# A Fourier-mixing and feed-forward block: which instruction takes a fresh pair of accumulator banks, and about 300 pieces at other places in the order

## The chip, the cores and the metric

One core of a Trainium2 chip runs one program. The metric is its time on the device in microseconds (us), as a median of several runs; beside it stands one profiled execution, whose rows are quoted throughout. Engines are named as in the profile: PE (TensorE: matrix products), DVE (VectorE), ACT (ScalarE), POOL (GpSimd), SP (SyncE: it issues transfers). The accumulators (PSUM) are eight banks of 128 x 512 floats; the kernel takes them in pairs, four pairs in all, one after another in turn.

## The reference

One transformer block in float32: a Fourier mixing layer and a feed-forward layer, each on a normalised input and each added to its input. x is 2048 x 512; the sequence matrices are 2048 x 2048, the hidden ones 512 x 512, w1 is 512 x 1792 and w2 1792 x 512.

```python
def _A_ref(x, dft_seq_re, dft_seq_im, dft_hid_re, dft_hid_im):
    a = jnp.einsum("bsd,ed->bse", x, dft_hid_re)
    b = jnp.einsum("bsd,ed->bse", x, dft_hid_im)
    return jnp.einsum("ts,bse->bte", dft_seq_re, a) - jnp.einsum("ts,bse->bte", dft_seq_im, b)

def _B_ref(x, w1, w2):
    h = _silu(jnp.einsum("bsd,df->bsf", x, w1))
    return jnp.einsum("bsf,fd->bsd", h, w2)

h = x + _A_ref(_layernorm(x), ...)
h2 = h + _B_ref(_layernorm(h), B_w1, B_w2)
```

## The kernel before, in words

**Arithmetic.** A float32 number is split in two parts of lower precision: ScalarE rounds it (`ph`, made at line 263), VectorE subtracts to get the remainder (`pl`, lines 267 and 269). Each product is then three matmuls into one bank: high x high, high x low, low x high (`three`, lines 313 to 315). The matrix products are made as Strassen-Winograd products: of a two-by-two block product, seven products (numbered 1 to 7 in the code) of sums of blocks, where VectorE makes the sums (line 711, `sub`) or a transfer adds on the way (`plus`, `prep`), and the results are added up partly in the banks and partly by VectorE.

**Stages.** The sequence transform comes first (`plain`, `fast`; banks `c` and `m`), for two halves of the output; `mix_fast` then multiplies by the hidden matrices (banks `y`), adds the residual (line 832) and calls `norm_h`, which normalises by way of a GpSimd reduction over partitions (line 903). `make_w2` splits the second layer's weights beforehand and stores them. Then, for each half q, `up` makes the first layer of the feed-forward part and `down` the second (banks `f`, weights fetched at line 1169).

**The first layer.** `up(q, ...)` goes over seven pairs p of hidden blocks. A pair has a bank Y (the first half of a bank pair `y`) and the banks V and X (the two halves of a bank pair `vx`). Products 1, 6, 5 and 3 go into Y, 7 and 4 into V, 2 into X. Product 1 is also needed as the start of X, so ScalarE copies Y into X when product 1 is done; product 2 then accumulates on it, and product 6 on Y. One product is six matmuls. The order is 1, 7, 6, 2, 5 for the first pair and, for every later one, 1, 7, 3 (of the pair before), 6, 2, 4 (of the pair before), 5. What follows each product (`post`) is on ScalarE or VectorE: `silu` (line 1065), `copy` (1068), `add` (1071), and the copy into X (1079).

**Order.** Nothing is ordered by hand in the text of the stages. Each stage appends pieces to a list `events`, every one with a planned time: matmul steps one behind another at 0.2265 us a matmul, other pieces at a lead before or a delay behind their step. The n-th piece appended has the number n. At the end the list is sorted by planned time plus the number that the table `MOVED` has for n:

```python
return sorted(((t + MOVED.get(n, 0.0), at, n, f) for t, at, n, f in events), key=lambda v: v[:3])
```

At the same time, what follows a step (0) comes before other pieces (1) and those before a step (2). In this order the instructions are traced, and each engine keeps the order in its own queue, SyncE's and GpSimd's transfers included. Buffers (51 pages of 128 x 1024 floats in SBUF, four pairs of banks) are handed out in the same order; the first instruction to use a buffer waits until its former contents have been read, and waits are put in from the order in which instructions use buffers. In the profile ScalarE's copy is the first to use a `vx` pair, since `post(1)` takes the pair and copies at once, and `post(1)` comes before the step of product 7, at the same planned time.

Pieces that the text speaks of, by number: 160 (the splits `S` of three sums of the input), 224 (the remainder of a hidden matrix, line 807), 269, 325, 629 and 696 (remainders `pl` of sequence blocks or their sums), 829 (transfers of parts of w2) and 830 (four subtractions on these, lines 1138 to 1141), 931 and 1247 (transfers of w1, line 991), 988 (the copy into X of the fifth pair, first half).

Of the kernel before, what the change touches and what calls it, by code (L numbers as in the profile page):

```python
# [42 lines left out]
FREE_US = {None: 2.0, "matmul": 4.0, "dma_start": 10.0}  # L43
LATE_SUMS = 2, 3, 4, 5, 6
# [200 lines left out]
def program(nc, page, keep, small, psum, dram, x, xT, seq, hid, ffn, out):  # L245
# [11 lines left out]
    def banks(name):  # L257
        return psum.tile([P, 2, 512], F32, tag="ps", name=name)
# [74 lines left out]
    X, xc, xraw = {}, {}, {}  # L333
# [713 lines left out]
    def up(q, lead, between):  # L1047

        bank = {}
# [9 lines left out]
        def mm(n, p):  # L1059
            if n == 1:  # L1060
                bank[p, "Y"] = banks(f"y{q}{p}")[:, 0, :]
            mul(n, p, n in (1, 7), n in (2, 6, 5, 3, 4))
# [323 lines left out]
```

## Time and profile before

| | |
|---|---|
| median of 3 runs | 685.56 us (684.73 to 687.5) |
| the profiled execution's own time | 684.68 us |
| its span, first to last instruction | 682.6 us |
| TensorE busy | 662.9 us, 97% of the span, 2892 matmuls |
| VectorE busy | 574.9 us, 84% |
| ScalarE busy | 372.0 us, 54% |
| mean granted TensorE clock | 0.999 |
| moved by transfers | 184.22 MB, mean 270 GB/s |

The span is what the rows of the trace cover; some 2 us of the device time lie around it. An engine is busy while one of its instructions runs; a matmul's row lasts longer than the distance to the next one, since matmuls overlap. Rows of a timeline are: start, duration, engine, line, operation, output and inputs, shapes, and in brackets the idle time of the engine before it with what ended it. In rows of a stretch each engine has its busy time and its number of instructions.

### The profile page before, as it was taken

What the parts mean: (1) busy time and instruction counts of PE and PEld (TensorE: products, weight loads), DVE (VectorE), ACT (ScalarE), POOL (GpSimd) and SP (SyncE); (2) the same over time, 40 slices, a digit from 0 to 9 for tenths busy, and PEclk for the clock granted to TensorE, in tenths of its full rate; (3) what the DMA queues carried; (4) which work ended last, traced back from release to release, by engine and by line L of the source; (5) the groups of instructions that cost most, each with busy time, mean ns of one, the idle gap of its engine ahead of it and who ended that gap; (6) DMA issues with size and microseconds to landing.
All of it is one profiled execution on the core that took longest, in us unless ns stands there. A gap on an engine that the chain in (4) does not pass through costs nothing.

```text
span 682.6 us, 8286 instructions
## 1 busy us (share of the span) xinstructions
PE 662.9 (97%) x2892; PEld 540.5 (79%) x2892; DVE 574.9 (84%) x727; ACT 372.0 (54%) x476; POOL 98.1 (14%) x128
## 2 busy tenths in 40 slices
PE   9999999999999999999999999989999999999996
PEld 6888887878888888888888877768888777778885
DVE  7899978998989999999999998967998545279874
ACT  6996555654545444455666446775455445554600
POOL 0010112120003233011201034341000000000000
PEclk9999999999999999999999999999999999999999
DMA  8975899999896769899999995459988562268803
GB/s 318 359 179 150 249 323 358 278 306 323 297 368 258 266 184 283 303 349 371 384 304 403 333 355 212 174 216 302 348 313 331 178 226 98 82 231 298 328 31 124
DMA packets 59706, 184.22 MB, mean 270 GB/s; under 512 B 6800, under 2 KB 13840, under 8 KB 59664
## 3 DMA queue, kind: packets, MB, share of 16 engines
q1 hardware_dynamic: 45456, 132.79, 53.7%
q0 software_dynamic: 13920, 50.63, 23.5%
q8 instruction: 23, 0.38, 0.2%
q10 hardware_dynamic: 288, 0.26, 0.1%
q14 instruction: 19, 0.16, 0.1%
HBM read 139.34 MB, written 44.32 MB: 269 GB/s over the span
## 4 chain that ended last, share of the span: by engine, by line
PE 87%; DVE 4%; DMA 3%; ACT 3%; issue 2%; SPq 0%; POOL 0%; DVEq 0%; ACTq 0%
PE m L314 8%; PE m L315 8%; PE m L313 8%; PE y L314 7%; PE y L315 7%; PE y L313 7%; PE f L315 6%; PE f L314 6%; PE f L313 6%; PE c L313 3%; PE c L314 3%; PE c L315 3%; PE vx L313 3%; PE vx L314 3%; PE vx L315 3%; DMA raw<-in_seq 3%
## 5 line engine op out<-in xcount | busy, mean ns | idle before, releaser
L263 ACT ACTIVATE ph<-raw 128x1024 fp32r<-128x1024 f32 x102 | 105.5, 1055 | 84.4 <-DVE raw L711 18.5
L267 DVE TENSOR_TENSOR pl<-raw,ph 128x1024 fp32r<-128x1024 f32 x88 | 109.0, 1257 | 7.9 <-ACT ph L263 7.4
L314 PE MATMUL m<-pl,S 128*128 128x512 f32 x192 | 74.8, 390 | 0.8 <-DVE pl L267 0.8
L315 PE MATMUL m<-ph,S 128*128 128x512 f32 x192 | 74.7, 389 | 0.0
L313 PE MATMUL m<-ph,S 128*128 128x512 f32 x192 | 74.7, 389 | 0.0
L313 PE MATMUL f<-gth,wf 128*128 128x512 f32 x161 | 62.6, 389 | 0.0
L314 PE MATMUL f<-gtl,wf 128*128 128x512 f32 x161 | 62.6, 389 | 0.0
L315 PE MATMUL f<-gth,wf 128*128 128x512 f32 x161 | 62.6, 389 | 0.0
L263 ACT ACTIVATE gth<-g 128x1024 fp32r<-128x1024 f32 x42 | 42.8, 1053 | 34.2 <-DVE g L1200 30.0
L1071 DVE TENSOR_TENSOR g<-vx,g 128x512 f32<-128x512 f32 x28 | 19.3, 690 | 48.3 <-PE vx L315 34.2
L314 PE MATMUL m<-pl,X 128*128 128x512 f32 x144 | 56.1, 390 | 1.0 <-DVE pl L267 1.0
L267 DVE TENSOR_TENSOR gtl<-g,gth 128x1024 fp32r<-128x1024 f32 x42 | 50.5, 1220 | 7.6 <-ACT gth L263 5.0
L315 PE MATMUL m<-ph,X 128*128 128x512 f32 x144 | 56.0, 389 | 0.0
L313 PE MATMUL m<-ph,X 128*128 128x512 f32 x144 | 56.0, 389 | 0.0
L711 DVE TENSOR_TENSOR raw<-raw,raw 128x1024 f32<-128x1024 f32 x36 | 47.8, 1331 | 1.6 <-DMA raw<-in_seq 1.3
L314 PE MATMUL y<-pl,hf 128*128 128x512 f32 x112 | 43.7, 390 | 0.0
L313 PE MATMUL y<-ph,hf 128*128 128x512 f32 x112 | 43.6, 389 | 0.0
L315 PE MATMUL y<-ph,hf 128*128 128x512 f32 x112 | 43.6, 389 | 0.0
L314 PEld LDWEIGHTS m<-pl,S 128*128 128x128 f32 x192 | 36.0, 188 | 8.9 <-DVE pl L267 1.4
L313 PEld LDWEIGHTS m<-ph,S 128*128 128x128 f32 x192 | 36.0, 188 | 7.5
L315 PEld LDWEIGHTS m<-ph,S 128*128 128x128 f32 x192 | 36.0, 188 | 7.4
L314 PEld LDWEIGHTS f<-gtl,wf 128*128 128x128 f32 x161 | 30.2, 188 | 6.3
(399 smaller groups left out, 1540.3 us busy)
## 6 DMA issues: line engine op xcount, KB each, us to landing
raw<-in_seq SPq DMA_DIRECT2D x84, 512.0 KB, 6.6
hf<-fd SPq DMA_DIRECT2D x28, 512.0 KB, 6.1
wf<-wd SPq DMA_DIRECT2D x28, 512.0 KB, 6.7
wf<-wd SPq DMA_DIRECT2D x28, 384.0 KB, 4.3
sf<-sd SPq DMA_DIRECT2D x18, 512.0 KB, 7.0
raw<-in_seq POOLq DMA_DIRECT2D x16, 512.0 KB, 6.9
fd<-hf POOLq DMA_DIRECT2D x14, 512.0 KB, 6.4
w<-in_ffn SPq DMA_DIRECT2D x23, 256.0 KB, 6.7
```

The source lines that it names most:

```text
L263: nc.scalar.activation(hi, src, AF.Copy, scale=sign)
L267: nc.vector.tensor_tensor(lo, src, hi, op=ALU.subtract)
L313: nc.tensor.matmul(acc, wh, mh, start=first, stop=False, skip_group_check=on)
L314: nc.tensor.matmul(acc, wh, ml, start=False, stop=False, skip_group_check=on)
L315: nc.tensor.matmul(acc, wl, mh, start=False, stop=last, skip_group_check=on)
L711: nc.vector.tensor_tensor(o, a, b, op=ALU.subtract)
L1071: nc.vector.tensor_tensor(g[q, f][:, tau, :], src, g[q, f][:, tau, :], op=ALU.add)
```

## The change

The pair of banks `vx` is taken when the step of product 7 is traced, by its first matmul, and no longer by ScalarE's copy. The copy of product 1 into X (`post(1)`) is planned 0.05 us behind product 1's end, so that it comes behind the step of product 7 in the order. Besides, 325 entries of `MOVED` have another value, come in or go out; the matmul steps have the same order as before.

```diff
+SEED_US = 0.05
...
         def mm(n, p):
             if n == 1:
                 bank[p, "Y"] = banks(f"y{q}{p}")[:, 0, :]
+            if n == 7:
+                t = banks(f"vx{q}{p}")
+                bank[p, "V"], bank[p, "X"] = t[:, 0, :], t[:, 1, :]
             mul(n, p, n in (1, 7), n in (2, 6, 5, 3, 4))
...
             if n == 1:
                 for i in range(2):
                     g[q, 2 * p + i] = page(f"g{q}{p}{i}")
-                t = banks(f"vx{q}{p}")
-                bank[p, "V"], bank[p, "X"] = t[:, 0, :], t[:, 1, :]
                 nc.scalar.activation(bank[p, "X"], bank[p, "Y"], AF.Copy)
...
-            after = [(0, lambda n=n, p=p: post(n, p))]
+            after = [(SEED_US if n == 1 else 0, lambda n=n, p=p: post(n, p))]
```

Of `MOVED`, the entries that the text speaks of (us, added to the planned time):

| piece | before | after |
|---|---|---|
| 160 | 27.45 | 21.61 |
| 224 | -0.48 | 9.8 |
| 269 | 7.52 | 1.26 |
| 325 | 7.54 | 5.83 |
| 629 | 0.53 | 7 |
| 696 | 6.8 | 7.94 |
| 829 | -0.65 | -10.88 |
| 830 | 0.56 | -11.76 |
| 931 | -77.43 | -54.39 |
| 988 | -0.38 | 2.42 |
| 1247 | none | -56.42 |

207 rows, old and new, of the table MOVED are left out of this document.

## The prediction

> **What bounds the kernel now.** I read the page's busy times first, then TensorE's waits, then the timeline around the commonest wait, then busy time by stage.
>
> ```profile
> PE 662.9 (97%) x2892; PEld 540.5 (79%) x2892; DVE 574.9 (84%) x727; ACT 372.0 (54%) x476; POOL 98.1 (14%) x128
> PEclk9999999999999999999999999999999999999999
> ...
> PE vx L313 <- ACT vx L1079: 11.0, 14, 1.5
> PE m L314 <- DVE pl L267: 1.8, 2, 1.0
> ...
> 200.00:300.00 100.00, 100.00 (x442) 82.65 (x442) 95.02 (x105) 49.59 (x53) 29.04 (x26) 1.00 0.82 275
> 300.00:400.00 100.00, 99.33 (x438) 81.72 (x438) 97.92 (x110) 56.76 (x63) 15.00 (x26) 1.00 1.00 358
> 400.00:500.00 100.00, 94.97 (x413) 76.70 (x412) 84.18 (x133) 61.06 (x88) 31.58 (x36) 1.00 0.74 269
> ```
>
> TensorE is the bound: 97% busy at full granted clock. It issues 442 matmuls in 100 us where nothing stops it, one each 0.226 us, so time can only come out of its gaps. Nearly all of them are one wait, 14 times, once for each pair of hidden blocks in each half of the first layer: the seventh product (`vx`) waits for ScalarE's copy at line 1079. Second comes VectorE: 95 to 98% busy from 200 to 400 us, so there a remainder (`pl`) that comes late is TensorE's next wait. Two such waits exist already.
>
> ```profile
> 404.06 0.39 PE L314 MATMUL y<-T1l,wah 128*128 128x512 f32 x1
> 404.29 0.39 PE L315 MATMUL y<-T1h,wal 128*128 128x512 f32 x1
> 404.72 0.58 ACT L1079 ACTIVATE vx<-y 128x512 f32<-128x512 f32 x1 [0.76 <-PE y L315]
> 405.35 0.50 PE L313 MATMUL vx<-T7h,sf 128*128 128x512 f32 x1 [0.67 <-ACT vx L1079]
> 405.69 0.39 PE L314 MATMUL vx<-T7l,sf 128*128 128x512 f32 x1
> ```
>
> This is one of the 14. The first product's last matmul starts at 404.29 and ends at 404.68, the copy runs from 404.72 to 405.30, and the seventh product starts at 405.35. The copy writes X, the product writes V, the other half of the same pair of banks: no data passes between them. The product waits because the copy is the first user of the newly taken pair.
>
> **The change, part by part.** *The 14 waits.* From 404.29 to 405.69 are 1.40 us for two issues that take 0.45 undisturbed: 0.95 lost, of which the waits view counts 0.67 as idle; the slow restart and the drain are 0.28 more. Over all, 11.0 + 14 x 0.28 = 14.9 us. Now the product takes the pair, and I expect the order of first users to turn round: the copy waits for the product's first matmul. That would start at 404.29 + 0.23 = 404.52 and end at 404.91; the copy would run from 404.95 to 405.53. The next matmul that needs the copy done is the sixth product, which accumulates on Y. In the first pair of each half it follows the seventh at once, at 404.52 + 6 x 0.226 = 405.88: 0.35 us to spare. In the other 12 the third product of the pair before lies between, and 1.7 us are spare. So I take all 14 waits as gone: -14.9.
>
> Two things could put some of it back. ScalarE works in order:
>
> ```profile
> 397.44 1.05 ACT L263 ACTIVATE T4h<-hn 128x1024 fp32r<-128x1024 f32 x1
> ...
> 457.63 0.62 ACT L1065 ACTIVATE g<-g 128x512 f32<-128x512 f32 x1
> ...
> 401.68 1.22 DVE L832 TENSOR_TENSOR h<-y,h 128x1024 f32<-128x1024 f32 x1
> ```
>
> An activation of 1.05 us that has just begun delays the copy by up to that, hidden 12 times by the 1.7 us, and costing up to 0.7 in each of the two first pairs. The long wait of 1.5 us was such a queue (the activation at 457.63 ahead of the copy). The copy of the fifth pair (piece 988, offset -0.38 to 2.42) now stands 2.47 us behind its first product, still ahead of the sixth product at 12 x 0.226 = 2.71. If the copy waits for the whole seventh product, it ends 0.58 + 0.04 after that one's end and the two first pairs stand as long as now: 2 x 0.95 = 1.9. Bounds for this term are 0 and +1.9; I take 0, for a wait at 404.72 came 0.04 us behind the one matmul it needed. What is late next in place of the copy is the bank itself: the second pair's banks are read last by the residual sum at 401.68, done at 402.90. That pair's product could now start at 404.52 less the 0.95 gained in the first pair, 403.57: 0.67 spare, nothing added.
>
> The Trainium skill (PSUM — Partial Sum Buffer, Terms) forbids two engines on one bank at one time, an error and not a delay. Copy and seventh product touch three different banks, so by that rule they may overlap and the term stays 0; were the pair guarded as one, it would be +1.9. The trace agrees only in part: the wait above exists between two different banks, so it comes from the program's hand-over of the pair.
>
> *The moved pieces.* 325 offsets differ; most shift work that has spare time. TensorE's own order of products is untouched. I compared the order of each queue in the two tables, SyncE's and GpSimd's loads and stores too, and looked for remainders that lose their lead.
>
> ```profile
> 112.70 1.22 DVE L267 TENSOR_TENSOR pl<-raw,ph 128x1024 fp32r<-128x1024 f32 x1
> 113.98 0.50 PE L314 MATMUL m<-pl,X 128*128 128x512 f32 x1 [1.01 <-DVE pl L267]
> ...
> 148.63 0.69 DVE L807 TENSOR_TENSOR hf<-hid,hf 128x512 fp32r<-128x512 f32 x1
> 149.23 1.22 DVE L267 TENSOR_TENSOR pl<-raw,ph 128x1024 fp32r<-128x1024 f32 x1
> ...
> 150.51 0.50 PE L314 MATMUL m<-pl,S 128*128 128x512 f32 x1 [0.83 <-DVE pl L267]
> ...
> 151.50 1.89 DVE L406 TENSOR_TENSOR S<-s,S 128x512 fp32r<-128x512 f32 x3
> ...
> 301.25 2.35 DVE L267 TENSOR_TENSOR pl<-raw,ph 128x1024 fp32r<-128x1024 f32 x2
> ...
> 305.72 0.39 PE L314 MATMUL m<-pl,X 128*128 128x512 f32 x1
> ...
> 315.88 0.43 DVE L1138 TENSOR_TENSOR v<-u,v 128x256 f32<-128x256 f32 x1 [1.58 <-DMA v<-in_ffn]
> ...
> 344.85 1.22 DVE L267 TENSOR_TENSOR pl<-raw,ph 128x1024 fp32r<-128x1024 f32 x1
> 345.99 0.95 DVE L406 TENSOR_TENSOR wal<-w,wah 128x768 fp32r<-128x768 f32 x1
> ...
> 346.52 0.39 PE L314 MATMUL m<-pl,X 128*128 128x512 f32 x1
> ```
>
> Each of the two old waits costs its idle time and 0.28: 1.29 and 1.11, mean 1.2. Piece 269, the remainder at 112.70, comes 6.3 us earlier (7.52 to 1.26): its wait goes, -1.3 (bounds -1.3 and 0). Piece 325, the one at 149.23, gets piece 160's three subtractions (1.89 us, 27.45 to 21.61) ahead of it and loses piece 224 (0.69, at 148.63, now 10.3 later): its wait grows by 1.2 (bounds 0 and 1.9). Piece 629, second of the two at 301.25, ends at 303.60 and is needed at 305.72, 2.1 spare; it moves 6.5 later (0.53 to 7), behind piece 830's four subtractions (the first at 315.88, which stood 1.58 waiting for its load), drawn 12.3 earlier with that load, piece 829. Piece 696, at 344.85, has 0.45 spare and gets the `wal` remainder ahead of it, whose load (piece 931) now starts 23 us later. For 629 and 696 no row shows the new order; the bounds are 0 (load early) and 1.9 (as for 325), and I take one ordinary wait each, 2 x 1.2 = 2.4.
>
> In the first layer VectorE was busy 84.18 of 100 us; about 7 pairs there lose 0.95 each, so it would be 84.18 of 93.4, 90%: below what 200 to 400 us carry at full TensorE. No term there.
>
> **Sum.** -14.9 + 0 - 1.3 + 1.2 + 2.4 = -12.6 us. The profiled execution took 684.68 us (span 682.6, 2.1 around it): 672.1. The median of the runs shown, 685.56, is 0.9 above it: 673.0. A change of 0.5%, 3.4 us, is about what a measurement here can tell from none.
>
> **The rivals.** *(A) The copy waits for the whole seventh product*, or ScalarE's queue holds it in the two first pairs: -12.6 + 1.9, so 674.9. For it: the pair is already handed over as one. Against: the first matmul alone is the first user.
>
> *(B) VectorE late all along.* With 95 and 98% from 200 to 400 us, eight more remainders of 1.2 us late give back 9.6: 682.6. For it: those shares, and offsets changed throughout. Against: the same work sits there as before, and only three pieces were found to lose their lead.
>
> ```profile
> 406.71 4.06 POOL L903 PARTITION_ALL_REDUCE m<-m  x1 [2.99 <-DMA u<-in_ffn]
> ...
> 407.59 2.46 DVE L1003 TENSOR_TENSOR ws<-w 128x256 f32<-128x256 f32 x1
> ...
> 409.98 0.41 DVE L1005 TENSOR_TENSOR ws<-w 128x256 f32<-128x256 f32 x1
> ```
>
> GpSimd's reduction adds 2.05 us (2.46 against 0.41) to the VectorE instruction it meets; several are moved, and a needed remainder behind one is late by that. The Trainium skill (SBUF — State Buffer, SBUF: two separate sides) says the port is locked for the whole instruction: 4.06 us by its rule, 2.05 by the trace, and the measured one stands.
>
> *(C) Slower: SyncE's queue held at the turn to the second layer.* Loads are issued in order, and one that waits for its page holds all behind it.
>
> ```profile
> SPq L991 <- PE vx L315: 35.9, 1, 35.9
> ...
> SPq L1169 <- DVE wS6l L267: 20.1, 1, 20.1
> wf<-wd SPq DMA_DIRECT2D x28, 512.0 KB, 6.7
> ```
>
> Piece 1247, a load of line 991 for the second half, moves 56 us forward, in among the loads of line 1169 that feed the second layer. A single wait there of 20 us, as seen, ahead of them decides from about 12.6 us beyond their lead on: 20 less a few us of lead is some 16, so 673.0 + 16 = 689. Against: the page it takes is freed by then in the order I worked out.
>
> *(D) The change does not do what it says*: the seventh product still waits for the copy or for the bank. Then -12.6 + 14.9 = +2.3: 688. Against: nothing passes from the copy to that product.
>
> **How the numbers follow.** Forecast 0.63, A 0.12, B 0.13, C 0.07, D 0.05. The predicted time is the forecast's, 673.0. Low end: all 14.9 and both old waits gone, none new, 685.56 - 17.3 = 668, 667.5 for round. High end: only the 11.0 of idle regained, 1.9 back, four late remainders of 1.2: -4.3, 681.3, and 682 so as to reach close to B; what is left out is half of B, C and D, some 0.18. Faster: forecast, A, and most of B, 0.86; within 0.5%: the rest of B with some of D, 0.07; slower: 0.07. Of the cases that are faster, 668 to 677 holds the likeliest one.
>
> **What would show it.** Right: TensorE's wait for line 1079's copy (1082 after) gone from its waits, the copy starting about 0.66 us behind the start of the first product's last matmul, first layer's pairs some 0.95 us shorter, and waits on `pl` two to four times at about 1 us. Wrong: a new wait of `y` on `vx` or `g` in every pair; `vx` waiting for VectorE's residual or `g`; more than six waits on `pl`; or a gap of several us at `f` with a load of line 1169 (1172 after) as its releaser.

## The result and the profile after

| | before | after |
|---|---|---|
| median | 685.65 us (684.73 to 687.5) | 670.22 us (670.08 to 670.99) |
| the profiled execution's own time | 684.68 us | 670.99 us |
| its span | 682.6 us | 669.2 us |

The ratio is 0.9774, with an interval of 0.9752 to 0.9795: 15.4 us by the medians, 13.7 between the two profiled executions, 13.4 between their spans. Predicted were 673.0 us, in 667.5 to 682. In the lines of after, the copy is at line 1082, the three matmuls at 315 to 317, a remainder at 269 or 271.

First the page's busy times and granted clock, then TensorE's waits (microseconds in total, times, longest), then busy time by stretch, all of the changed kernel:

```profile
PE 659.8 (99%) x2892; PEld 541.6 (81%) x2892; DVE 578.3 (86%) x727; ACT 369.5 (55%) x476; POOL 97.1 (15%) x128
PEclk9999999999999999999999999999999999999999
...
PE y L315 <- ACT vx L1082: 1.7, 2, 1.0
PE m L316 <- DVE pl L269: 1.4, 2, 1.0
...
300.00:400.00 100.00, 97.91 (x430) 80.09 (x429) 97.66 (x109) 55.77 (x62) 15.93 (x27) 1.00 1.02 370
400.00:500.00 100.00, 100.00 (x443) 82.73 (x442) 91.03 (x138) 63.01 (x91) 28.79 (x34) 1.00 0.75 267
...
```

TensorE's 14 waits of `vx` for the copy are gone. From 400 to 500 us it now issues 443 matmuls without a stop, where it had issued 413, and VectorE is 91.03% busy there. What is left of TensorE's waits is 1.7 us for the copy, two times, and 1.4 us for remainders, two times, besides 1.6 us at the start of the run, where before had 1.5. The first kind was not forecast. The timeline of the changed kernel at the first pair of feature blocks, at the second, and at the first of the other half:

```profile
396.51 0.39 PE L317 MATMUL y<-T1h,wal 128*128 128x512 f32 x1
...
397.87 0.39 PE L317 MATMUL vx<-T7h,sf 128*128 128x512 f32 x1
398.30 0.58 ACT L1082 ACTIVATE vx<-y 128x512 f32<-128x512 f32 x1 [3.00 <-PE vx L317]
...
398.93 0.50 PE L315 MATMUL y<-T6h,sf 128*128 128x512 f32 x1 [0.67 <-ACT vx L1082]
399.26 0.39 PE L316 MATMUL y<-T6l,sf 128*128 128x512 f32 x1
...
405.64 0.39 PE L317 MATMUL vx<-T7h,sf 128*128 128x512 f32 x1
405.86 0.39 PE L315 MATMUL y<-T3h,sf 128*128 128x512 f32 x1
406.06 0.58 ACT L1082 ACTIVATE vx<-y 128x512 f32<-128x512 f32 x1 [2.12 <-PE vx L317]
...
407.22 0.39 PE L315 MATMUL y<-T6h,sf 128*128 128x512 f32 x1
...
533.54 0.50 PE L315 MATMUL y<-T6h,sf 128*128 128x512 f32 x1 [1.01 <-ACT vx L1082]
```

The copy (398.30) starts behind the *last* of the seventh product's six matmuls (397.87), 1.79 us behind the start of the first product's last one (396.51), not 0.66. The sixth product has to wait for it, 0.67 us idle; in the other half, 1.01. In the second pair the copy is as late (406.06), but the third product of the pair before fills TensorE until the sixth starts at 407.22, and nothing is lost. In the other eleven pairs of this kind it is the same: the copy starts 0.43 to 0.49 us behind the start of the seventh product's last matmul and ends 0.52 to 0.58 us ahead of the sixth product. So in 12 of 14 pairs the lateness is hidden and in two it shows.

The two other waits, with what VectorE did just before:

```profile
302.80 0.43 DVE L1144 TENSOR_TENSOR u<-u,v 128x256 f32<-128x256 f32 x1
303.14 1.22 DVE L269 TENSOR_TENSOR pl<-raw,ph 128x1024 fp32r<-128x1024 f32 x1
...
304.41 0.50 PE L316 MATMUL m<-pl,X 128*128 128x512 f32 x1 [0.46 <-DVE pl L269]
...
343.23 0.95 DVE L408 TENSOR_TENSOR wal<-w,wah 128x768 fp32r<-128x768 f32 x1
...
344.10 1.22 DVE L269 TENSOR_TENSOR pl<-c,ph 128x1024 fp32r<-128x1024 f32 x1
345.23 1.22 DVE L269 TENSOR_TENSOR pl<-raw,ph 128x1024 fp32r<-128x1024 f32 x1
...
346.50 0.50 PE L316 MATMUL m<-pl,X 128*128 128x512 f32 x1 [0.96 <-DVE pl L269]
```

Both are where the prediction put them. The remainder at 303.14 stands directly behind the four subtractions (the last at 302.80), and the one at 345.23 two places behind `wal` (343.23).

To add up such stops in every kernel below, I use the distance from one matmul's start to the next. Undisturbed it is 0.2265 us; a stop adds the excess, and the next distance is long too, by 0.11. The first wait above is 1.06 - 0.23 + 0.11 = 0.94 us for 0.67 idle. Summed over one profiled execution of each kernel, in us (for e5 it is another execution of the changed kernel):

| kernel | start, to 10 | 10 to 395 (remainders) | 395 to 610 (first layer) | all | span |
|---|---|---|---|---|---|
| before | 2.55 | 2.50 | 14.84 (14 waits) | 19.9 | 682.6 |
| after | 2.89 | 2.07 | 2.23 (2) | 7.2 | 669.2 |
| e1 claim only | 2.60 | 4.42 | 3.08 (3) | 10.1 | 672.7 |
| e2 copy first | 2.40 | 1.87 | 14.86 (14) | 19.1 | 681.7 |
| e3 X beside Y | 2.45 | 2.68 | 17.13 (15) | 22.3 | 684.7 |
| e4 no cover | 2.93 | 0.82 | 15.45 (15) | 19.2 | 681.9 |
| e5 after again | 2.97 | 0.92 | 2.24 (2) | 6.1 | 667.9 |
| e6 two remainders earlier | 2.80 | 0.95 | 1.95 (2) | 5.7 | 667.5 |
| e7 cover, second half | 2.48 | 2.59 | 0.95 (1) | 6.0 | 667.9 |
| e8 both | 3.72 | 0.97 | 0.95 (1) | 5.6 | 667.3 |
| e9 copy inside the seventh | 2.65 | 1.60 | 2.23 (2) | 6.5 | 668.4 |

Span less losses is 661.7 to 662.7 us in all eleven: these stops account for the time to within 1 us. Between before and after they are 12.7 of the 13.4 us.

### The profile page after: what moved, and what is told of

It is laid out like the page before. It is cut to its first block, busy times and chain, and to the rows that moved or that the text cites. A ratio compares the mean times of both kernels' runs of the same rounds, so it can differ in the third digit from the quotient of the medians.

```text
span 669.2 us, 8292 instructions
## 1 busy us (share of the span) xinstructions
PE 659.8 (99%) x2892; PEld 541.6 (81%) x2892; DVE 578.3 (86%) x727; ACT 369.5 (55%) x476; POOL 97.1 (15%) x128
## 5 line engine op out<-in xcount | busy, mean ns | idle before, releaser
L269 DVE TENSOR_TENSOR pl<-raw,ph 128x1024 fp32r<-128x1024 f32 x88 | 111.4, 1288 | 6.0 <-ACT ph L265 4.3
L713 DVE TENSOR_TENSOR raw<-raw,raw 128x1024 f32<-128x1024 f32 x36 | 45.7, 1273 | 1.0 <-DMA raw<-in_seq 0.4
```

The costliest lines, as they stand in the source:

```text
L269: nc.vector.tensor_tensor(lo, src, hi, op=ALU.subtract)
L713: nc.vector.tensor_tensor(o, a, b, op=ALU.subtract)
```

## The experiments

Two theories stood at the start. Theory 1: the gain is the claim's, and what is left of the copy's cost comes from the pair of banks being handed over as one piece, for readers as for writers. Theory 2 differs by run: the moved pieces carry the gain, or only the pair's first user matters and the copy is late for another reason.

Some of the expectations below call the product that waits in the first pairs the second, and count 400 moved pieces: by the trace it is the sixth (`T6h`), and the pieces are 325.

**The claim alone (e1), the order alone (e2).**

```diff
 e1, against the changed kernel: MOVED as before, and
+MOVED.update({988: -0.02, 1036: -0.02})
 e2, against the changed kernel:
                 t = banks(f"vx{q}{p}")
                 bank[p, "V"], bank[p, "X"] = t[:, 0, :], t[:, 1, :]
+                nc.scalar.activation(bank[p, "X"], bank[p, "Y"], AF.Copy)
...
                     g[q, 2 * p + i] = page(f"g{q}{p}{i}")
-                nc.scalar.activation(bank[p, "X"], bank[p, "Y"], AF.Copy)
```

> The claim of the pair by the seventh product and ScalarE's copy behind that product, with the order of the pieces as the kernel before has it (only the two copies of pieces 988 and 1036 stand directly behind their product, at -0.02). Theory 1 (the claim carries the gain): TensorE's stalls at the seventh product go, 14.8 us by the pitches of the trace before, and the first pairs' two waits for the copy come instead, 2.2 us, so about 12.6 us under the kernel before, 672 to 674 us; the two waits for VectorE's remainders near 114 and 150 us stay (2.4 us) and the two near 304 and 346 us are absent (2.0 us). Theory 2 (the 400 moved pieces carry a good part, and with the old order the claim meets late pieces): the copy's place is not enough, several new waits of TensorE in 400 to 610 us, 676 us or more.

> The changed kernel's order of pieces, but the copy of the first product stands ahead of the seventh product's matmuls again, so that the seventh product adds to it. Theory 1 (the claim carries the gain): 14 waits of the seventh product for the copy come back at about 1.05 us each, 14.8 us, and the first pairs' two waits of the second product (2.2 us) go: 670.2 + 12.6 = 682.8 us, 681 to 684. Theory 2 (the order carries a good part): 676 us or less.

Measured: e1 674.0 us, ratio 0.9827 (0.9798 to 0.9856), 11.2 us under before by the medians and 11.9 by the ratio; e2 683.35 us, ratio 0.9973 (0.9953 to 0.9993), 1.8 us under it, with an interval of 0.5 to 3.2. The two together are 13.0 to 13.7 us; the whole change was 15.4. In e2 the 14 waits are back with the row that the prediction read in before. Its waits, and the seventh product in the second pair:

```profile
PE vx L315 <- ACT vx L1067: 11.0, 14, 1.4
...
404.61 0.50 PE L315 MATMUL vx<-T7h,sf 128*128 128x512 f32 x1 [0.67 <-ACT vx L1067]
```

So theory 1 holds: the claim carries 11 to 12 of 15 us. By e2 the order carries about 2 of the rest; where these come from is shown in part only. One part shows in the first layer. TensorE's waits of e1, a late chain near 325 us, and ScalarE's queue ahead of the fifth pair's copy:

```profile
PE y L315 <- ACT vx L1082: 2.3, 3, 0.9
PE m L315 <- ACT c L682: 1.7, 1, 1.7
PE m L316 <- DVE pl L269: 1.6, 2, 1.0
...
317.91 0.43 DVE L1141 TENSOR_TENSOR v<-u,v 128x256 f32<-128x256 f32 x1 [4.66 <-DMA v<-in_ffn]
...
324.17 1.09 ACT L682 ACTIVATE c<-m 128x512 f32<-128x512 f32 x2 [1.27 <-DVE Vl L1154]
...
325.31 0.50 PE L315 MATMUL m<-ph,X 128*128 128x512 f32 x1 [1.66 <-ACT c L682]
...
436.34 1.06 ACT L1153 ACTIVATE Vh<-v 128x1024 fp32r<-128x1024 f32 x1 [1.76 <-DVE v L1143]
...
437.31 1.04 ACT L265 ACTIVATE wS5h<-ws 128x1024 fp32r<-128x1024 f32 x1
...
438.25 0.58 ACT L1082 ACTIVATE vx<-y 128x512 f32<-128x512 f32 x1
...
438.88 0.50 PE L315 MATMUL y<-T6h,wS4h 128*128 128x512 f32 x1 [0.86 <-ACT vx L1082]
```

The copy of piece 988 stood here behind two activations of 1.06 and 1.04 us; it came at 438.25 and cost the sixth product 0.86 idle. In the changed kernel the piece is planned 2.4 us later and no wait is seen there. Ahead of 395 us e1 has before's order and lost 4.42 us against 2.50, and this difference is not the order's. One stop at 325.31 that before had not is 1.94 of it. It goes back to VectorE's subtraction at 317.91, which waited 4.66 us for its load; in before it came at 315.88 after 1.58. The order is the same, the load was issued 1.04 us earlier than in before (306.23 against 307.27) and landed 2 us later, and everything behind it in VectorE's queue was 2.04 us later, the activation at 324.17 too. The remainder of piece 696 was as late as that (346.89 against 344.85) and stopped TensorE at 348.16, 0.84 us lost, where no wait was expected. The wait near 150 us, which was expected to stay, is not there.

**Is the pair guarded as one piece? X beside Y (e3).**

```diff
-                bank[p, "Y"] = banks(f"y{q}{p}")[:, 0, :]
+                t = banks(f"y{q}{p}")
+                bank[p, "Y"], bank[p, "X"] = t[:, 0, :], t[:, 1, :]
             if n == 7:
-                t = banks(f"vx{q}{p}")
-                bank[p, "V"], bank[p, "X"] = t[:, 0, :], t[:, 1, :]
+                bank[p, "V"] = banks(f"vx{q}{p}")[:, 0, :]
```

> The copy's half moves: X now lies beside Y in the first product's pair of banks, and V alone in the seventh product's. Theory 1 (a pair of banks is guarded as one piece, for readers and writers on other engines, however the halves are used): the copy no longer waits for the whole seventh product, so the first pairs' two waits go (2.2 us); but the matmuls that add to X or Y next wait for every copy out of that pair, so in each pair of feature blocks the product that adds to Y or X again stalls for the ScalarE copy out of the pair (about 14 to 16 waits of about 0.95 us): 670.2 - 2.2 + 15 = 683 us, 680 to 686. Theory 2 (each bank is guarded by itself, and the copy only waited for the seventh product because that product claimed the pair): no such waits, 668 us.

Measured: 686.42 us in one run, 16.2 above after. The waits, and the second pair:

```profile
PE y L315 <- ACT g L1073: 11.6, 13, 1.4
PE y L315 <- ACT g L1070: 1.4, 2, 0.7
...
410.11 0.60 ACT L1073 ACTIVATE g<-y 128x512 f32<-128x512 f32 x1 [0.81 <-PE y L317]
...
410.75 0.50 PE L315 MATMUL y<-T2h,wah 128*128 128x512 f32 x1 [0.74 <-ACT g L1073]
```

The wait for the whole seventh product is gone, and 15 others are there: the second product (410.75), which adds to X, waits for ScalarE to have read Y (410.11), the other half of the pair. No data passes between those two either. A reader of one bank thus holds up a writer of the other. The time is above the forecast 683, and 0.4 above the forecast's upper end, in part because a stop cost 1.14 us on the mean (17.13 / 15) and not 0.95: in three pairs an activation of 1.05 or 1.06 us stood ahead of the copy on ScalarE. One late remainder near 346 us cost another 2.1 us.

**The same inside a product (e9).** In the first pairs, the copy stands between the halves of the seventh product.

```diff
+            if n == 7 and p == 0:
+                mul(n, p, True, False, (0,))
+                nc.scalar.activation(bank[p, "X"], bank[p, "Y"], AF.Copy)
+                mul(n, p, True, False, (1,))
+                return
```

> In the two first pairs of feature blocks, ScalarE's copy of the first product stands between the two halves of the seventh product (behind three of its six matmuls). Theory 1 (the pair of banks is guarded as one piece, also inside a product): the copy starts behind the third matmul, the fourth waits for the copy, and the second product's two waits near 399 and 534 us turn into waits of the same size inside the seventh product, so the time stays at 669.5 to 671 us. Theory 2 (only the whole seventh product's end was waited for, as the pair's first user): the copy ends while the seventh product runs on in its own bank, no wait in either place, 2.2 us less: 668 us.

Measured: 670.15 us in one run. Its waits and the first pair:

```profile
PE vx L315 <- ACT vx L1069: 1.7, 2, 1.0
...
396.35 0.39 PE L317 MATMUL vx<-T7h,sf 128*128 128x512 f32 x1
396.78 0.58 ACT L1069 ACTIVATE vx<-y 128x512 f32<-128x512 f32 x1 [1.16 <-PE vx L317]
...
397.41 0.50 PE L315 MATMUL vx<-T7h,sf 128*128 128x512 f32 x1 [0.67 <-ACT vx L1069]
...
398.21 0.39 PE L315 MATMUL y<-T6h,sf 128*128 128x512 f32 x1
```

The copy came behind the third matmul (396.35), the fourth (397.41) waited for it with the same 0.67 us, and the sixth product (398.21) no longer did. The stop moved with the place in the order and kept its size; that is what theory 1 said, and theory 2 is out. The first user plays no part in it: whatever stands earlier in the order and touches the pair is waited for.

**Is it the third product that hides the other 12 copies? (e4)** With this order the copy of the fifth pair in the first half falls behind the sixth product and takes that product in as well, which changes what this pair computes; this pair has no wait for the copy.

```diff
-            order += [(n, p - (n in (3, 4))) for n in (1, 7, 3, 6, 2, 4, 5)]
+            order += [(n, p - (n in (3, 4))) for n in (1, 7, 6, 3, 2, 4, 5)]
```

> In the pairs of feature blocks behind the first, the sixth product stands directly behind the seventh and the third of the pair before behind the sixth (1, 7, 6, 3, 2, 4, 5 in place of 1, 7, 3, 6, 2, 4, 5). Theory 1 (the copy is late in every pair, and the third product of the pair before hides it in twelve of fourteen): the product that adds to the copy or to its pair now follows the seventh product too closely, so up to 12 more waits of TensorE for the copy, 0.95 to 1.1 us each: about 11 to 13 us, 681 to 683 us. Theory 2 (the copy waits only for the first product, and has long ended when the pair is used again): no more waits than the changed kernel's two, 670 us.

Measured: 683.74 us in one run. The waits and the second pair:

```profile
PE y L315 <- ACT vx L1082: 9.1, 13, 0.7
...
404.39 0.39 PE L317 MATMUL vx<-T7h,sf 128*128 128x512 f32 x1
404.82 0.58 ACT L1082 ACTIVATE vx<-y 128x512 f32<-128x512 f32 x1 [2.12 <-PE vx L317]
...
405.45 0.50 PE L315 MATMUL y<-T6h,sf 128*128 128x512 f32 x1 [0.67 <-ACT vx L1082]
```

Eleven more waits for the copy, 13 in all, each with the shape of the first pairs': copy at 0.43 us behind the start of the seventh product's last matmul, product six 0.63 behind the copy's start. Two other stops, at 443.88 and 447.05, are 2.7 us of the 15.45; they were not forecast, and the time is 0.7 us above the 681 to 683 that were. In the changed kernel the copy is late in every pair; the third product is the cover.

**Can the rest be had? (e5 to e8)** These ran on one chip: the changed kernel again, the two remainders earlier, a cover for the second half's first copy, and both.

```diff
 e6
+MOVED.update({628: 7.0, 629: 5.6, 696: 6.9})
 e7
+MOVED.update({1255: 1.359, 1256: 1.359, 1257: 1.359, 1258: 1.359, 1259: 1.359,
+              1260: 1.359, 1261: 3.119, 1266: -4.077})
 e8: both
```

In the changed kernel 628, 629 and 696 are 8.53, 7 and 7.94. Piece 1266 is the first product of the next pair, pieces 1255 to 1260 the sixth, second and fifth of the first, with what follows each.

> The changed kernel itself, beside the three variants of it, so that they can be compared with it on the same chip. Theory: 670.2 us, 669.5 to 671.5, with the second product's two waits for the first pairs' copies (idle 0.7 to 1.0 us each, near 399 and 534 us), and the remainders' waits near 304 and 346 us anywhere from 0 to 2 us each, since they hang on when VectorE's work ahead of them was released.

> Two places in the order put right: the remainder of piece 629 ahead of the four operations of VectorE that make the sums for the second matrix, and that of piece 696 ahead of the residual's. Theory 1 (both waits come from VectorE's order): the waits near 304 and 346 us go, 0.73 and 1.23 us by the pitches of the changed kernel, so 1.9 us under it: 668.3 us. Theory 2 (VectorE is late there because of what was released late, or the work put behind is now late itself): 669.5 to 671 us with a wait of TensorE for another remainder or for the residual's output instead.

> In the second half's first pair of feature blocks, the first product of the next pair is put between the seventh and the sixth product, so that the copy has another product to hide behind, as in the later pairs it has the third of the pair before. Theory 1 (the copy's wait is for the whole seventh product, and six matmuls cover it): the wait near 534 us goes, 1.3 us by the pitches, 668.9 us, and the one near 399 us stays. Theory 2 (the copy ends late for another reason, ScalarE's own order): the wait moves to the sixth product or to the next pair's seventh, 670 us or more.

> Both edits together: the two remainders earlier on VectorE, and the next pair's first product as cover for the second half's first copy. Theory 1: 1.9 + 1.3 us under the changed kernel, 667.0 us (666 to 668), with one wait of the kind left, near 399 us. Theory 2 (one of the two gives nothing): 668.3 to 669.

| kernel | median | from to | ratio to before | expected |
|---|---|---|---|---|
| e5 | 669.82 us | 669.34 to 673.02 | 0.9759 (0.9729 to 0.9789) | 670.2 |
| e6 | 669.06 us | 668.62 to 670.46 | 0.9741 (0.9710 to 0.9772) | 668.3 |
| e7 | 669.65 us | 669.10 to 669.78 | 0.9746 (0.9718 to 0.9773) | 668.9 |
| e8 | 668.53 us | 667.76 to 669.18 | 0.9730 (0.9703 to 0.9758) | 667.0 |

All gave less than theory 1 said: 0.8, 0.2 and 1.3 us under e5 for 1.9, 1.3 and 3.2. The runs of e6 and of e7 overlap with those of e5, so for neither alone is a gain of the whole time shown. For e7 the profile shows that the edit did its part. The timeline of e7, a remainder's wait and then the first pair of the second half:

```profile
346.49 0.50 PE L317 MATMUL m<-pl,X 128*128 128x512 f32 x1 [1.40 <-DVE pl L270]
...
532.20 0.39 PE L318 MATMUL vx<-T7h,sf 128*128 128x512 f32 x1
532.43 0.39 PE L316 MATMUL y<-T1h,wah 128*128 128x512 f32 x1
...
532.98 0.58 ACT L1083 ACTIVATE vx<-y 128x512 f32<-128x512 f32 x1 [2.04 <-PE vx L318]
...
533.79 0.39 PE L316 MATMUL y<-T6h,sf 128*128 128x512 f32 x1
```

The seventh product's last matmul (532.20) is followed by the next pair's first product (532.43), the copy (532.98) ends behind that, and the sixth product starts at 533.79 without a wait. The first layer's losses are 0.95 in place of 2.24 us, 1.3 as expected. But the same execution stopped 1.40 us for a remainder at 346.49, where e5 had no stop; nothing of the edit lies there. The table has it: 2.59 us lost ahead of 395 us, against 0.92. For the other runs of e7 there is no trace, so its gain is shown for the stage and not for the whole time.

For e6 both waits are gone (e5 had only the first, 0.92 us) and another has come. VectorE in e5, and VectorE and TensorE in e6:

```profile
350.74 1.22 DVE L269 TENSOR_TENSOR pl<-raw,ph 128x1024 fp32r<-128x1024 f32 x1
```

```profile
301.14 1.23 DVE L270 TENSOR_TENSOR pl<-raw,ph 128x1024 fp32r<-128x1024 f32 x1 [0.94 <-ACT ph L266]
...
352.01 1.22 DVE L270 TENSOR_TENSOR pl<-raw,ph 128x1024 fp32r<-128x1024 f32 x1
...
353.28 0.50 PE L317 MATMUL m<-pl,X 128*128 128x512 f32 x1 [0.67 <-DVE pl L270]
```

The remainder that came at 350.74 in e5 came at 352.01 in e6, and TensorE, which had not needed to wait for it, stopped 0.67 us. Theory 2 of that run was right, in both its parts. Piece 629, moved forward, came up on VectorE (301.14) before ScalarE had its input ready, and the whole queue stood 0.94 us; with a second wait of this kind, 0.50 us at 326.25, it was 0.96 us behind e5 at 341.68, ahead of the place where 696 was moved, and 1.27 behind it. VectorE, 98.08% busy there, did not make this up. And TensorE, no longer stopped near 304 us, wanted the remainder sooner.

e8 is the fastest kernel of the study: its slowest run, 669.18 us, is below the fastest of e5, 669.34. It is 1.3 us, 0.2%, better than the changed kernel.

## Why the prediction came out right

**The 14 waits, -14.9: right.** By the distances they were 14.84 us and all are gone; e2 brings them back at 14.86. That the idle time undercounts a stop, 11.0 against 14.9, held.

**The copies of the two first pairs, 0: wrong, and the rival's bound was the truth.** Measured is +2.23 for the bound of +1.9, since the second half's stop is 1.28 in place of 0.95. There the copy started 0.76 us behind the start of the seventh product's last matmul and not 0.42. The step that failed is "I expect the order of first users to turn round: the copy waits for the product's first matmul". e9 and e3 show what stands in its place: the copy waits for everything earlier in the order that touches the pair, six matmuls, and readers count as well. The reason given for 0, that a copy came 0.04 us behind the one matmul it needed, was read from before, where the copy *was* the pair's first user and there was nothing else to wait for; such a row couldn't tell the two apart. The same holds for "all 12 others are hidden": right in number, but by 0.52 to 0.58 us and not by the 1.7 the prediction gave (in the second pair the copy runs to 406.64, the sixth product starts at 407.22), and e4 shows what hangs on it.

The Trainium skill (PSUM — Partial Sum Buffer, PSUM bank collisions raise a hardware error) advises to guard by bank and quadrant. This kernel guards two banks together: 15 stops of e3 lie between different banks. A program that guards each bank by itself would by that rule lose none of these; no run here shows it, and it was not tried.

**Piece 269, -1.3: right.** No wait is left near 114 us in the changed kernel; the remainder comes at 107.37 there. e2 and e7, with the same order, lost 0.56 and 0.41 us near 116, for a later remainder (piece 273).

**Piece 325, +1.2: wrong, its wait went too**, so -1.1. I counted what stood directly ahead of it in the queue and not when that queue started. VectorE in before, some 6 us ahead of this remainder, and piece 325 in e1:

```profile
142.75 2.48 DVE L711 TENSOR_TENSOR raw<-raw,raw 128x1024 f32<-128x1024 f32 x2 [1.26 <-DMA raw<-in_seq]
```

```profile
147.96 1.22 DVE L269 TENSOR_TENSOR pl<-raw,ph 128x1024 fp32r<-128x1024 f32 x1
```

In before, VectorE stood 1.26 us for a load, and all behind it was late by that, piece 325 (149.23) too. In e1, with before's order, VectorE did not wait there (141.48), piece 325 came 1.27 us earlier, and TensorE had no wait at 150 us. The changed kernel did not wait there either (140.91), and piece 325 came at 147.10, with the three subtractions ahead of it. So the wait that the prediction let grow came from a load that was late in one execution, and the 1.1 us are no gain that the new order is shown to bring.

**Pieces 629 and 696, +2.4: right in place, 1.96 in size** (0.73 and 1.23). But these sizes are of one execution. In six others with the same order ahead of 395 us (e2, e3, e4, e5, e7, e9), the sum of all stops there was 0.82 to 2.68 us; in all seven, piece 629 cost 0 to 0.92 and piece 696 0 to 2.1. And 696 cost 0.84 in e1 with the old order, for a late load, so how much of its stop is the new order's stays open.

**The sum.** Predicted -12.6, found -14.84 + 2.23 - 1.28 - 1.11 + 1.96 = -13.0. It came close because two errors of about 2.2 us cancel: the first pairs cost 2.2 more, and piece 325 cost 2.3 less. That was luck. Of the 2.8 us between 673.0 and 670.22, 0.4 is that sum, 0.4 the rest of the span's 13.4, 0.3 the difference between span and time, and 1.7 where the profiled executions lie: the median stood 0.9 above the profiled one before, and 0.8 below it after.

**The rivals.** A's mechanism came true, at 2.2 us; the time landed by the forecast because of piece 325. B, many remainders late, did not: two stops, not eight. Its reason did show, though, in e6, where time won on two remainders was lost in part at a third. C: TensorE's waits name no load of the second layer. D: excluded by the 14 waits that are gone, and by e2, where the 14 waits come back with the copy ahead of the product.

The moved pieces, costed at +2.3 in all, were worth -1.8 in e2 (interval -3.2 to -0.5). The losses ahead of 395 us point the same way, 2.50 and 4.42 in two executions with the old order, 0.82 to 2.68 in seven with the new one, but they overlap, and late loads are part of the first two. Which of the 325 entries did it is not shown.

The Trainium skill (Perfetto Trace Analysis, Optimization Strategy) reads a gap that repeats on the engine that should be saturated as a possible sign of too few buffers. Here 14 such gaps of 0.67 us and more went away with the number of banks unchanged; who stood first in the order was the cause.

## What to carry to other kernels

Where one buffer is cut into halves for two purposes, ask who is made to wait for whom by the handing over of the whole, not by the data: here a copy into one bank and a product into the other held each other up either way round, and the gain came from putting the wait where other work covers it. The cover is to be named and its spare time worked out for each place (here the third product, 0.5 to 0.6 us to spare, missing in two of fourteen pairs). And a stop of about 1 us behind an engine that is 95% busy is not a fixed price: look at several executions before building a term on it.

## What was not expected of the hardware

A stop of TensorE costs 0.27 to 0.28 us beyond its idle time over a wide range of lengths (0.46 idle cost 0.73, 1.40 cost 1.67), at a granted clock of 0.998 to 1.000. Of that, 0.16 is the end of the matmul before: the idle time is counted from its row's end, 0.39 us behind its start, where the next would have started 0.2265 behind it. The other 0.11 is the start again: the first matmul behind a stop takes 0.50 in place of 0.39 us, and the next follows 0.34 behind it. So twenty short stops are worth more than their idle time says.

The same load for the same subtraction made VectorE wait 1.58 us in one execution and 4.66 in another with the same order ahead of it. That alone moved TensorE's losses by 2.8 us, 1.94 at 325.31 and 0.84 at 348.16, more than the edits of e6 to e8 gained. Why the load took longer is not shown.
